# Attention and two feed-forward layers on one core: early tiles and weight pieces in another order, and a block's first products behind all reads of their PSUM tile

## Chip, core and metric

The kernel runs on one core of a Trainium2 chip. The metric is the device time of one execution in microseconds; the median of three runs before the change is 1276.29 us.

## What is computed

The reference takes q, k and v of shape (8, 8, 576, 64). It does three things, one after the other:

```python
# 1. attention inside chunks of 64 positions
attn = softmax(q_c @ k_c.T / 8); out = attn @ v_c
x = out.transpose(0, 2, 1, 3).reshape(8, 576, 512)
# 2. norm, two products with a ReLU between, residual (w_ch1: 512 x 2048, w_ch2: 2048 x 512)
xn = (x - mean) / sqrt(var + 1e-6) * g_ln
x = x + relu(xn @ w_ch1) @ w_ch2
# 3. product, gelu, norm of one half, mixing along the sequence, gate, product, residual
h = gelu(x @ w_in); u, v = halves of h
x = x + (u * (w_sg @ norm(v) + b_sg)) @ w_out
```

## The kernel before, in words

The 4608 rows of x are 36 tiles of 128 rows. Steps 1 and 2 run first, for all tiles; step 3 follows. The change touches steps 1 and 2 alone.

**Tiles and blocks.** attention(t) makes one tile: two loads (q and k, then v), products of 64x64 (L295), row maxima, exponential, transposes (L305), products with v (L314), and the division (L344), which writes x. norm(t) makes the normed tile and splits it into a high half (16 bits, scalar engine, L381) and a low half (the rest, L383), which a DMA transpose writes to xT. Two tiles make a block; there are 18 blocks (NB) of 256 rows.

**Weights.** w1 and w2 come in 8 pieces each (j = 0 to 7), stored as 64-bit numbers: load_raw() loads a piece of 1 MB (two buffers, `straw`), f64() makes 32-bit numbers of it (L398 on the scalar engine, L403 on the vector engine). For w1, make_w1() finds the largest value (L424 on the scalar engine or absmax on the vector engine), sends it over all partitions with two tiny products (par(): L206, L218), scales the piece (L446 on the scalar engine or L452 on GpSimd) and splits it into halves w1h (L457) and w1l (L459). For w2 the halves are made once all 8 maxima are there (scale_w2, split_w2).

**Products.** Every product is three products of 16-bit halves (high x high, high x low, low x high). ff1(b, f) is one of 16 units of the first layer for block b, 12 products at L536, read out by L540 and L541; a w1 piece feeds two units of each block, so four while blocks 0 and 1 are done together. ff2(b, f) (L557) is the second layer. These plain forms serve blocks 0 to 3. Blocks 4 to 17 use ff1p and ff2p (L640 and L689), which save products by sums and differences of quarters: ff2p(b, j) makes seven groups of three products, P1, P6, P5, P7, P2, P3, P4 in this order, each in a half bank of PSUM. P1 and P6 are the two halves of one bank, P5 and P7 those of another, and both banks are one tile, pair[0]. P2 and P3 share a bank (bank[6]), P4 lies in bank[7]. All seven add up over the eight units j = 0 to 7 of a block; then copy(1), stt(6), copy(5), stt(7) and stt(2), stt(3), stt(4) read them out (copy is L712 on the scalar engine, stt is L707 on the vector engine), and the unit j = 0 of the next block starts the same banks again.

**What sets the order.** All of this is not issued as written. Each step is given to a planner by op(engine, ns, function, rd, wr, prio, lat). run() keeps a clock for each engine, takes the step that can start first, the one with the smallest prio among those that are ready, and issues it; ns is the time that the planner believes a step takes, lat what it adds before another engine may use the result. So the table TUNE (the prio of tiles in `a`, of w1 pieces in `w`, of w2 pieces in `w2`; the engine of steps in `lo`, `wl`, `wc`, `wa`, `wm`) and the numbers ns set the order of the instructions of each engine, and the hardware runs each engine's list in that order. Where the planner sees TensorE idle before a step, busy() issues products of a tile of zeros (L970), whose result nobody reads. The waits between engines are put in by the framework from what each instruction reads and writes, in the order in which they were issued. It follows whole tiles: a write to any part of pair[0] waits for the reads of pair[0] that were issued ahead of it, and a read waits for the writes that were issued ahead of it.

## Time and profile before

| | |
|---|---|
| three runs | 1274.23, 1276.29, 1277.38 us; median 1276.29 |
| the profiled execution | 1274.01 us, span 1272.2 us, mean granted TensorE clock 0.993 |
| busy: TensorE, vector, scalar, GpSimd | 96%, 65%, 46%, 39% of the span |
| steps 1 and 2; step 3 | up to 866.95 us; from there to the end |
| first product of the first layer | 38.62 us |

The trace has one row for each instruction or for a few equal ones: start and length in microseconds, engine, line, what is written and read, and in brackets the idle time of the engine just before it with what ended it. PE is TensorE, DVE the vector engine, ACT the scalar engine, POOL GpSimd, SP the engine that issues the DMAs. A product on PE is shown as busy until its last result is out, so products that follow each other closely overlap in the rows, and the sum of a stretch can hide small losses.

### The profile page before, as it was taken

To read this page: it belongs to the slowest core of one execution; us is meant where nothing else is said; L and a number is where in the kernel's file an instruction comes from. 1 tells how busy PE (TensorE), PEld (TensorE's weight loads), DVE (VectorE), ACT (ScalarE), POOL (GpSimd) and SP (SyncE) were. 2 spreads that over 40 slices of the span, in tenths; PEclk is the share of its full clock that TensorE was granted. 3 is DMA by queue.
4 is the path that set the end of the run, shared out by engine and by line. 5 is a ranking of instruction groups with operands and counts; after the bars stand their busy time and mean duration, and the time that the engine had idled before them with its cause. 6 is when DMAs were issued, how large, how long until landed. Compare 5 with 4: busy or idle time off the path is not lost.

```text
span 1272.2 us, 26588 instructions
## 1 busy us (share of the span) xinstructions
PE 1218.5 (96%) x11119; PEld 872.5 (69%) x11119; DVE 825.1 (65%) x1621; ACT 586.5 (46%) x963; POOL 491.2 (39%) x446
## 2 busy tenths in 40 slices
PE   6889999988999999999999999999999999999998
PEld 4677654667888888888888888884544554554553
DVE  7885125995766656555555665546979579669665
ACT  5775402545834533333334333535736626526530
POOL 3341401644656544434444344233434144233220
PEclk9999999989999999999999999999999999999999
DMA  9954002246312221222132120612030331331102
GB/s 303 261 172 120 1 26 67 74 149 181 101 51 68 51 73 48 66 67 67 52 67 60 51 59 18 156 28 91 9 68 33 116 59 42 125 59 42 50 1 75
DMA packets 106392, 102.05 MB, mean 80 GB/s; under 512 B 79648, under 2 KB 79648, under 8 KB 106272
## 3 DMA queue, kind: packets, MB, share of 16 engines
q1 hardware_dynamic: 106272, 100.36, 28.2%
q8 instruction: 87, 1.43, 0.5%
q14 instruction: 33, 0.27, 0.1%
HBM read 62.59 MB, written 18.87 MB: 64 GB/s over the span
## 4 chain that ended last, share of the span: by engine, by line
PE 75%; DVE 14%; ACT 3%; DMA 3%; POOL 2%; issue 2%; SPq 0%; DVEq 0%; ACTq 0%; POOLq 0%
PE bank L640 20%; PE pair L689 11%; PE bank L689 8%; PE pb L1105 8%; PE pb L1087 7%; PE pb L1167 6%; PE pair L557 3%; PE pb L1043 3%; PE bank L536 3%; PE bank L557 2%; DMA straw<-in_w 2%; DVE gl L249 1%; PE pair L295 1%; DVE tf L600 1%; PE pb L1106 1%
## 5 line engine op out<-in xcount | busy, mean ns | idle before, releaser
L640 PE MATMUL bank<-xT,w1h 128*128 128x256 f16 x1792 | 301.6, 273 | 0.0
L689 PEld LDWEIGHTS <-arena 128*128 128x128 f16 x2352 | 226.7, 98 | 46.0 <-issue 17.0
L640 PE MATMUL bank<-xT,w1l 128*128 128x256 f16 x896 | 245.0, 273 | 0.0
L669 POOL TENSOR_TENSOR arena<-arena 128x896 f16<-128x896 f32 x69 | 130.2, 1886 | 255.6 <-ACT arena L667 255.5
L667 ACT ACTIVATE arena<-arena 128x896 f16<-128x896 f32 x112 | 106.3, 949 | 204.7 <-PE bank L689 131.4
L640 PEld LDWEIGHTS <-w1h 128*128 128x128 f16 x1792 | 175.3, 98 | 21.7 <-issue 0.5
L662 DVE TENSOR_TENSOR arena<-arena 128x256 f32<-128x256 f32 x112 | 63.6, 568 | 149.1 <-ACT arena L655 146.9
L655 ACT ACTIVATE arena<-bank 128x512 f32<-128x512 f32 x112 | 66.6, 595 | 123.7 <-PE bank L640 122.5
L689 PE MATMUL pair<-w2s,arena 128*128 128x256 f16 x672 | 110.6, 274 | 10.3 <-DVE u L707 6.8
L689 PE MATMUL pair<-w,arena 128*128 128x256 f16 x672 | 111.0, 274 | 2.7 <-DVE u L707 1.3
L1119 POOL TENSOR_TENSOR uT<-uT,vs 128x512 f32<-128x512 f32 x32 | 49.0, 1533 | 151.6 <-DVE vs L1115 151.6
L1043 PE MATMUL pb<-win,x2T 128*128 128x512 f16 x432 | 96.8, 379 | 1.5 <-DVE x L707 1.5
L640 PEld LDWEIGHTS <-w1l 128*128 128x128 f16 x896 | 87.9, 98 | 10.4
L1087 PE MATMUL pb<-x2T,win 128*128 128x384 f16 x576 | 94.6, 326 | 0.0
L689 PE MATMUL bank<-w,arena 128*128 128x256 f16 x672 | 93.7, 274 | 0.0
L536 PE MATMUL bank<-xT,w1h 128*128 128x256 f16 x512 | 86.1, 273 | 6.7 <-DVE latel L541 2.9
L1105 PE MATMUL pb<-wsg,vh 128*128 128x512 f16 x288 | 88.0, 380 | 0.0
L1167 PE MATMUL pb<-wout,gh 128*128 128x512 f16 x288 | 85.7, 379 | 1.9 <-DVE x L1172 1.9
L1087 PEld LDWEIGHTS <-win 128*128 128x128 f16 x576 | 56.2, 98 | 37.5
L717 POOL TENSOR_TENSOR x<-x,u 128x256 f32<-128x256 f32 (+1 forms) x60 | 64.4, 1089 | 44.3 <-ACT arena L667 30.8
L1024 DVE SCALAR_TENSOR_TENSOR q<-q,h 128x384 f32<-128x384 f32 (+1 forms) x84 | 51.3, 614 | 39.0 <-ACT q L1022 39.0
L1043 PEld LDWEIGHTS <-x2T 128*128 128x128 f16 x432 | 41.3, 98 | 50.9 <-issue 2.7
(225 smaller groups left out, 2332.5 us busy)
## 6 DMA issues: line engine op xcount, KB each, us to landing
straw<-in_w SPq DMA_DIRECT2D x16, 1023.8 KB, 6.6
qkl<-in_qkv SPq DMA_DIRECT2D x26, 512.0 KB, 3.8
x2d<-x SPq DMA_DIRECT2D x36, 256.0 KB, 2.0
x<-x2d SPq DMA_DIRECT2D x36, 256.0 KB, 4.4
out<-x SPq DMA_DIRECT2D x36, 256.0 KB, 2.0
vl<-in_qkv SPq DMA_DIRECT2D x26, 256.0 KB, 2.7
qk<-in_qkv SPq DMA_DIRECT2D x10, 512.0 KB, 5.7
raw<-in_w_in SPq DMA_DIRECT2D x4, 1023.8 KB, 5.6
```

Source lines behind the costliest of these rows:

```text
L536: nc.tensor.matmul(acc, lhsT=w[j][:, k, fc], rhs=xT.t[:, x, k], start=(n == 0), stop=(n == 11))
L557: nc.tensor.matmul(acc[i], lhsT=h[x].t[:, c], rhs=w2t[j][:, f % 2, y], start=(f == 0 and n == 0), stop=(f == NF - 1 and n == 2),)
L640: nc.tensor.matmul(acc[:, y * 256:y * 256 + 256], lhsT=w[j][:, k, fc], rhs=xT.t[:, x, k], start=(n == 0), stop=(n == 11),)
L655: op("ACT", 600, lambda: nc.scalar.activation(out=o.t[:, 0:4].rearrange("p n t -> p (n t)"), in_=acc, func=AF.Relu, scale=0.5), rd=[kb] + ...
L667: op("ACT", 950, lambda: nc.scalar.activation(out=h.t[:, 0], in_=o.t[:, 1:8], func=AF.Copy), rd=[o] + ar, wr=[h], prio=-100)
L669: op(lo[0], lo[1], lambda: lo[2].tensor_tensor(out=h.t[:, 1], in0=o.t[:, 1:8], in1=h.t[:, 0], op=ALU.subtract), rd=[o], wr=[h], prio=-100)
L689: nc.tensor.matmul(acc, lhsT=h.t[:, x, n], rhs=r(y), start=(first and j == 0 and m == 0), stop=(j == 7 and m == 2), skip_group_check=True,)
L717: op("POOL", ns, lambda: nc.gpsimd.tensor_tensor(out=d(), in0=d(), in1=v(), op=ALU.add), rd=u, wr=[x], prio=-50)
L1043: nc.tensor.matmul(ps, lhsT=x[:, k, c], rhs=w[:, k, 512:1024], start=(n == 0), stop=(n == 11))
L1087: nc.tensor.matmul(ps, lhsT=w[:, k, fc], rhs=x[:, k, c], start=(n == 0), stop=(n == 11))
L1105: nc.tensor.matmul(ps, lhsT=v[:, fc], rhs=w[:, 0:512], **f)
L1167: nc.tensor.matmul(ps, lhsT=x[:, k, c], rhs=w[:, k], start=(n == 0), stop=(n == 11))
```

## The change

It has four parts, all of them in what the planner is told.

1. Other numbers in TUNE: other prio of tiles 0 to 7 and of all weight pieces, and other engines. The scaling of w1 pieces 3, 4 and 7 moves from the scalar engine to GpSimd (`wc`); the low halves of pieces 2, 3 and 6 move from the vector engine to GpSimd and that of 7 the other way (`wl`); the maximum of w1 piece 2 moves to the scalar engine (`wa`); of the w2 maxima those of pieces 0, 3 and 7 change their engine, so that five instead of six are on the vector engine (`wm`); the low halves of tiles 4, 6 and 7 move to the vector engine (`lo`).
2. Other believed times ns (the first tiles now use the table COST too).
3. OWN: the first product of a block, P1 at j = 0, is also a write of P6, P5 and P7 to the planner, and P2 one of P3. So it stands behind all four reads of pair[0].
4. The reads of a block's sums are given other dependencies among each other (the names q1, q6, q5, q7), without the long lat of 1200.

```diff
-    a=[-270, -85, -10, -65, -85, -10, -145, 0],
+    a=[-465, -3175, 30, -50, -95, 25, -3470, 1760],
...
-    wl=[0, 0, 1, 1, 0, 0, 1, 0],
-    wc=[0, 1, 0, 0, 0, 1, 1, 0],
+    wl=[0, 0, 0, 0, 0, 0, 0, 1],
+    wc=[0, 1, 0, 1, 1, 1, 1, 1],
...
-            if not early:
-                ns = COST.get((eng, ns), ns)
+            ns = COST.get((eng, ns), ns)
...
-        op("ACT", 260, lambda: nc.scalar.activation(out=h[0].t, in_=acc, func=AF.Relu), rd=[kb], wr=[h[0]], prio=-100)
+        op("ACT", 370, lambda: nc.scalar.activation(out=h[0].t, in_=acc, func=AF.Relu), rd=[kb], wr=[h[0]], prio=-100)
...
+    OWN = {1: ["P6", "P5", "P7"], 2: ["P3"]}
...
-            op("PE", 326, lambda p=p: mm(p), rd=[h, f"w2_{j}"], wr=[f"P{p}"] + extra, prio=1000 + nff[0])
+            op("PE", 326, lambda p=p: mm(p), rd=[h, f"w2_{j}"], wr=[f"P{p}"] + extra + OWN.get(p, []) * (j == 0), prio=1000 + nff[0])
...
-            def stt(p, c, out, add, n=0):
+            def stt(p, c, out, add, x, rd=()):
...
-                ), rd=[f"P{p}", f"P{3 if p == 2 else p}"], wr=u if n else [x1 if p == 4 else x0], prio=-120, lat=1200)
+                ), rd=[f"P{p}", *rd], wr=[x], prio=-120)
...
-            copy(1, ca, 0)
-            stt(6, cb, lambda: U(1), lambda: U(0), 1)
-            copy(5, cb, 2)
-            stt(7, cb, lambda: U(3), lambda: U(1), 3)
+            copy(1, ca, 0, ["P1", "P6"], u + ["q1"])
+            stt(6, cb, lambda: U(1), lambda: U(0), "q6", ["q1"])
+            stt(7, cb, lambda: U(3), lambda: U(1), "q7", ["q6"])
+            copy(5, cb, 2, ["P5", "P7", "q1"], ["q5"])
```

The lines of the changed kernel are shifted: L689 is L690 there, L707 is L708, L712 is L713, and lines between about 240 and 670 are one less.

Three places show what moves. The first is TensorE around a boundary of two blocks (from block 8 to 9). pair_63 is the tile pair[0], w_7 and w_0 are pieces of w2, w2s are sums made of them; P1 and P5 read w, P6 and P7 w2s; L314 (L313) belongs to a tile of attention. Before:

```order
L689 MATMUL pair_63<-w2s_2496,arena 128x256
L314 MATMUL pair_64<-vl,pt 64x64 [waits DMAHW7_49,Activation_49]
L689 MATMUL pair_63<-w_7_166,arena 128x256 [waits Activation_49]
...
L689 MATMUL pair_63<-w_0_159,arena 128x256 [waits Activation_49]
...
L689 MATMUL pair_63<-w2s_2489,arena 128x256 [waits DVE_49]
```

Now:

```order
L313 MATMUL pair_64<-vl,pt 64x64 [waits DMAHW7_49,Activation_49]
...
L690 MATMUL pair_63<-w_7_166,arena 128x256
...
L690 MATMUL pair_63<-w2s_2552,arena 128x256 [waits Activation_49]
...
L690 MATMUL pair_63<-w_0_159,arena 128x256 [waits DVE_49]
...
L690 MATMUL pair_63<-w2s_2545,arena 128x256
```

In the last unit of the old block the attention product stood between P6 and P5, and P5 waited for copy(1); now it stands ahead of P1, and P7 waits for copy(1). In the new block P6 waited for the vector engine (stt(7), issued behind P1); now P1 does, and P6 waits for nothing. The first pattern stands at seven boundaries (from block 8 to block 15), the second at all 13.

The second place is the vector engine at the same kind of boundary. Before, stt(7) stood last, behind a step of the next block (L669):

```order
L707 SCALAR_TENSOR_TENSOR u<-pair_63,c_c2b,u 128x256 [waits Activation_49]
L707 SCALAR_TENSOR_TENSOR x<-bank_67,c_c2a,x 128x256 [waits PE_49]
L707 SCALAR_TENSOR_TENSOR x<-bank_68,c_c2n,x 128x256 [waits PE_49]
L707 SCALAR_TENSOR_TENSOR x<-bank_67,c_c2a,x 128x256
L669 TENSOR_TENSOR arena<-arena 128x896 [waits Activation_49]
L707 SCALAR_TENSOR_TENSOR u<-pair_63,c_c2b,u 128x256 [waits PE_49,Activation_49]
```

```order
L708 SCALAR_TENSOR_TENSOR u<-pair_63,c_c2b,u 128x256 [waits PE_49,Activation_49]
L708 SCALAR_TENSOR_TENSOR u<-pair_63,c_c2b,u 128x256 [waits Activation_49]
L708 SCALAR_TENSOR_TENSOR x<-bank_67,c_c2a,x 128x256 [waits PE_49]
L708 SCALAR_TENSOR_TENSOR x<-bank_68,c_c2n,x 128x256 [waits PE_49]
L708 SCALAR_TENSOR_TENSOR x<-bank_67,c_c2a,x 128x256
L668 TENSOR_TENSOR arena<-arena 128x896 [waits Activation_49]
```

Now the two reads of pair[0] stand first and next to each other, and stt(7) no longer waits for TensorE's product of the new block.

The third place is GpSimd in the first part (w1l is the low half of a w1 piece, hl that of a tile, cw<-cw the scaling of a piece). Before:

```order
L452 TENSOR_SCALAR cw_334<-cw_334,gsw_139 128x256 x4
...
L459 TENSOR_TENSOR w1l1_152<-cw_334,w1h1_144 128x1024
L383 TENSOR_TENSOR hl_591<-xn_581,hl_591 128x512
L459 TENSOR_TENSOR w1l0_151<-cw_271,w1h0_143 128x1024
...
L459 TENSOR_TENSOR w1l4_155<-cw_788,w1h4_147 128x1024
...
L452 TENSOR_SCALAR cw_878<-cw_878,gsw_139 128x256 x4
L459 TENSOR_TENSOR w1l5_156<-cw_878,w1h5_148 128x1024
```

Now:

```order
L451 TENSOR_SCALAR cw_386<-cw_386,gsw_139 128x256 x4
L458 TENSOR_TENSOR w1l1_152<-cw_386,w1h1_144 128x1024
L458 TENSOR_TENSOR w1l0_151<-cw_309,w1h0_143 128x1024
...
L451 TENSOR_SCALAR cw_685<-cw_685,gsw_139 128x256 x4
L451 TENSOR_SCALAR cw_887<-cw_887,gsw_139 128x256 x4
L458 TENSOR_TENSOR w1l3_154<-cw_685,w1h3_146 128x1024
L451 TENSOR_SCALAR cw_947<-cw_947,gsw_139 128x256 x4
L458 TENSOR_TENSOR w1l4_155<-cw_887,w1h4_147 128x1024
```

The low halves of pieces 1 and 0 now follow each other directly, and from piece 3 on GpSimd scales each piece as well as halving it, with the scaling of the next piece ahead of the low half of this one. The number of products with zeros on TensorE goes from 55 to 108.

## Rows read from the trace of the kernel before

**Rows 1.** The page: span, and busy time of TensorE and the vector engine.

```profile
span 1272.2 us, 26588 instructions
PE 1218.5 (96%) x11119; PEld 872.5 (69%) x11119; DVE 825.1 (65%) x1621; ACT 586.5 (46%) x963; POOL 491.2 (39%) x446
```

**Rows 2.** Waits of TensorE: total us, times, longest.

```profile
PE pair L689 <- DVE u L707: 8.1, 12, 1.0
PE pair L295 <- DVE x L344: 8.1, 5, 2.6
...
PE pair L689 <- DVE x L707: 0.6, 1, 0.6
```

**Rows 3.** Stretches: length, busy time of PE, PEld, DVE, ACT, POOL, granted clock.

```profile
0.00:38.62 38.62, 25.95 (x432) 18.59 (x433) 28.18 (x63) 23.39 (x43) 16.51 (x28) 0.91 0.97 311
38.62:45.33 6.71, 4.57 (x93) 3.65 (x90) 6.21 (x18) 2.25 (x6) 4.40 (x6) 1.00 1.01 160
45.33:126.50 81.17, 72.76 (x758) 60.40 (x759) 60.30 (x136) 57.14 (x121) 20.93 (x21) 1.00 0.58 174
126.50:220.00 93.50, 93.50 (x590) 52.26 (x588) 26.08 (x49) 21.68 (x35) 17.35 (x13) 1.00 0.11 32
```

**Rows 4.** TensorE: all products with zeros as a group, and one row of ten.

```profile
L970 PE MATMUL bank<-zero 128*128 128x256 bf16 x55 | 11.3, 358 | 1.9 <-DVE zero L875 1.0 <-issue 0.9
...
46.65 1.25 PE L970 MATMUL bank<-zero 128*128 128x256 bf16 x10
```

**Rows 5.** Timeline of all engines at one boundary of blocks, 566 to 574 us.

```profile
566.66 0.49 PE L689 MATMUL pair<-w,arena 128*128 128x256 f16 x3
...
566.99 0.49 PE L689 MATMUL pair<-w2s,arena 128*128 128x256 f16 x3
...
567.52 0.47 ACT L712 ACTIVATE u<-pair,c_c2a 128x256 f32<-128x256 f32 x1
...
568.04 0.49 PE L689 MATMUL pair<-w,arena 128*128 128x256 f16 x3
...
572.30 0.49 PE L689 MATMUL pair<-w,arena 128*128 128x256 f16 x3
...
572.90 0.48 DVE L707 SCALAR_TENSOR_TENSOR u<-pair,c_c2b,u 128x256 f32<-128x256 f32 x1 [1.00 <-PE pair L689]
...
573.44 0.49 PE L689 MATMUL pair<-w2s,arena 128*128 128x256 f16 x3 [0.65 <-DVE u L707]
```

**Rows 6.** TensorE, two places where P7 waits for copy(1).

```profile
300.24 0.49 PE L689 MATMUL pair<-w2s,arena 128*128 128x256 f16 x3 [1.76 <-ACT u L712]
...
787.55 0.49 PE L689 MATMUL pair<-w2s,arena 128*128 128x256 f16 x3 [0.56 <-ACT u L712]
```

**Rows 7.** Groups up to 125 us, vector and scalar engine: busy us, mean ns.

```profile
L459 DVE TENSOR_TENSOR w1l<-cw,w1h 128x1024 f16<-128x1024 f32 x3 | 3.7, 1222 | 1.1 <-ACT w1h L457 1.0
L201 DVE TENSOR_REDUCE mxw<-cw 128x4 f32<-128x1024 f32 x3 | 3.6, 1194 | 0.0
L432 DVE TENSOR_TENSOR mxw<-mxw,g1s 128x4 f32<-128x4 f32 x3 | 1.7, 556 | 0.0
...
L446 ACT ACTIVATE cw<-cw,gsw 128x256 f32<-128x256 f32 x20 | 8.5, 498 | 1.3 <-DVE gsw L440 1.3
```

**Rows 8.** Timeline of GpSimd and, last, of the vector engine, 27 to 38 us.

```profile
27.71 1.85 POOL L452 TENSOR_SCALAR cw<-cw,gsw 128x256 f32<-128x256 f32 x4 [1.73 <-DVE gsw L440]
...
34.19 1.15 POOL L383 TENSOR_TENSOR hl<-xn,hl 128x512 f16<-128x512 f32 x1
35.30 2.13 POOL L459 TENSOR_TENSOR w1l<-cw,w1h 128x1024 f16<-128x1024 f32 x1
...
36.09 1.37 DVE L432 TENSOR_TENSOR mxw<-mxw,g1s 128x4 f32<-128x4 f32 x1
```

**Rows 9.** Timeline of SP: issues of the last eight loads of weights.

```profile
68.40 31.19 SPq L391 DMA_DIRECT2D straw<-in_w  x7
102.21 0.37 SPq L391 DMA_DIRECT2D straw<-in_w  x1
```

More of the change, by code (lines that the diff above doesn't have):

```diff
@@ L397, in f64 @@
         dst = dst or (lambda: w.t)
-        op("ACT", 950 if pr < 9000 else 1350, lambda: nc.scalar.activation(
+        op("ACT", 1350, lambda: nc.scalar.activation(
             out=top.t.bitcast(F16).rearrange("p (n w) -> p n w", w=2)[:, :, 1],
@@ L402, in f64 @@
         ), rd=[raw], wr=[top], prio=pr)
-        op("DVE", 1140, lambda: nc.vector.scalar_tensor_tensor(
+        op("DVE", 1210, lambda: nc.vector.scalar_tensor_tensor(
             out=dst().bitcast(U32), in0=raw.t.rearrange("p (n w) -> p n w", w=2)[:, :, 0], scalar=13,
@@ L440, in scale @@
             nc.vector.tensor_scalar(out=gs, in0=g1s, scalar1=inv, scalar2=8.0, op0=ALU.mult, op1=ALU.mult)
-        op("DVE", 520, scale, wr=[f"e{j}"], prio=pr)
+        op("DVE", 690, scale, wr=[f"e{j}"], prio=pr)
         def mul():
@@ L456, in make_w1 @@
         op(("ACT", "POOL")[TUNE['wc'][j]], (1620, 1840)[TUNE['wc'][j]], mul, rd=[f"e{j}"], wr=[w], prio=pr)
-        op("ACT", 950, lambda: nc.scalar.activation(out=w1h[j], in_=wv(), func=AF.Copy), rd=[w], wr=[f"w1h{j}"], prio=pr)
+        op("ACT", 1050, lambda: nc.scalar.activation(out=w1h[j], in_=wv(), func=AF.Copy), rd=[w], wr=[f"w1h{j}"], prio=pr)
         lo = ("DVE", 1140, nc.vector) if TUNE['wl'][j] else ("POOL", 2100, nc.gpsimd)
@@ L539, in ff1 @@
         op("PE", 1285, mm, rd=[xT, f"w1h{j}", f"w1l{j}"], wr=[kb], prio=pr)
-        op("ACT", 260, lambda: nc.scalar.activation(out=h[0].t, in_=acc, func=AF.Relu), rd=[kb], wr=[h[0]], prio=-100)
-        op("DVE", 340, lambda: nc.vector.scalar_tensor_tensor(
+        op("ACT", 370, lambda: nc.scalar.activation(out=h[0].t, in_=acc, func=AF.Relu), rd=[kb], wr=[h[0]], prio=-100)
+        op("DVE", 415, lambda: nc.vector.scalar_tensor_tensor(
             out=h[1].t, in0=acc, scalar=0.0, in1=h[0].t, op0=ALU.max, op1=ALU.subtract
@@ L704, in ff2p, with copy @@
             U = lambda n: u[n // 2].t[:, n % 2 * 256:n % 2 * 256 + 256]
-            def stt(p, c, out, add, n=0):
+            def stt(p, c, out, add, x, rd=()):
                 op("DVE", 480, lambda: nc.vector.scalar_tensor_tensor(
                     out=out(), in0=POS[p][0], scalar=c, in1=add(), op0=ALU.mult, op1=ALU.add
-                ), rd=[f"P{p}", f"P{3 if p == 2 else p}"], wr=u if n else [x1 if p == 4 else x0], prio=-120, lat=1200)
-            def copy(p, c, n):
-                op("ACT", 380, lambda: nc.scalar.activation(
+                ), rd=[f"P{p}", *rd], wr=[x], prio=-120)
+            def copy(p, c, n, rd, wr):
+                op("ACT", 470, lambda: nc.scalar.activation(
                     out=U(n), in_=POS[p][0], func=AF.Copy, scale=c
-                ), rd=[f"P{p}", f"P{p + 5 if p == 1 else 7}"], wr=[u[n // 2]], prio=-120, lat=1200 if n else 300)
+                ), rd=rd, wr=wr, prio=-120)
             def add(x, d, v, ns):
@@ L718, in add @@
                     out=d(), in0=d(), in1=v(), op=ALU.add
[L719 to L732 removed]
+                ), rd=u + ["q6", "q5", "q7"], wr=[x], prio=-50)
+            copy(1, ca, 0, ["P1", "P6"], u + ["q1"])
+            stt(6, cb, lambda: U(1), lambda: U(0), "q6", ["q1"])
+            stt(7, cb, lambda: U(3), lambda: U(1), "q7", ["q6"])
+            copy(5, cb, 2, ["P5", "P7", "q1"], ["q5"])
+            stt(2, ca, lambda: half(x0, 0), lambda: half(x0, 0), x0, ["P3"])
+            stt(3, ca, lambda: half(x0, 1), lambda: half(x0, 1), x0)
+            stt(4, cn, lambda: half(x1, 0), lambda: half(x1, 0), x1)
+            add(x0, lambda: x0.t, lambda: u[0].t, 1400)
+            add(x1, lambda: half(x1, 0), lambda: U(3), 850)
+            add(x0, lambda: half(x0, 1), lambda: U(2), 850)
+            add(x1, lambda: half(x1, 1), lambda: U(3), 850)
+            add(x1, lambda: half(x1, 1), lambda: U(2), 850)
             for t, x in ((2 * b, x0), (2 * b + 1, x1)):
```

23 lines of the change are left out of this document (7 added, 16 removed).

## The prediction

> **What bounds the kernel now.** I read the page's busy shares first: TensorE is busy for 1218.5 of 1272.2 us, no other engine over 65% [rows 1]. So I looked next at what TensorE waits for, summed by cause [rows 2], and then at where those waits lie, by a table of stretches [rows 3]. The reader should see three things. First, the total idle time of TensorE is only 53.7 us; a change of order can win no more than that, plus part of the 11.3 us in which TensorE multiplies the tile of zeros [rows 1, 4]. Second, one cause repeats: the first products of a block (L689) wait for the vector engine's reading of the block before (L707), 8.1 us in 12 waits and 0.6 us once more [rows 2]. Third, the rest is early: 12.7 us idle before the first real product at 38.62 us, 2.1 us up to the first product of block 1 at 45.33, 8.4 us from there to 126.5, and none from 126.5 to 220 [rows 3, 4].
>
> The granted clock is 0.91 in the stretch to 38.62 us and 1.00 in the three behind it [rows 3], so the loss from the lower level of TensorE's clock (1.2 instead of 2.4 GHz) lies there too.
>
> **The boundaries of the blocks.** There are 13 (blocks 5 to 17). Rows 5 show one. P1, the first product of the new block, starts at 572.30; only behind it may stt(7), the last read of the old block's sums in the same tile, run (572.90), and only behind that P6 (573.44): TensorE sits idle for 0.65 us. In the changed order P1 itself stands behind all reads, P6 no longer waits, and nothing is left between stt(7) and P1: in that row set copy(1) starts at 567.52, and the four reads take 0.47 or 0.48 us each, so with gaps of about 0.1 they end near 570, over 2 us ahead of P1. The 13 waits are worth 8.7 us idle. Each also breaks the overlap of groups: a group of three is busy for 0.49 us, but they follow each other by 0.33 (566.66, 566.99) [rows 5], so 0.16 us more is lost each time, 2.1 us in all. **Gain: 10.8 us.**
>
> The order shows what is given back. Before, in seven boundaries an attention product (L314) stands between P6 and P5 of the last unit, and the wait of P5 for copy(1) passes underneath it: 567.52 + 0.47 is 567.99, P5 starts at 568.04, with no idle time [rows 5]. Now that product stands ahead of P1, and the wait for copy(1) has moved to P7 of the same unit, with nothing to cover it. A row has this price: where P7 waits for copy(1) already, the idle time is 0.56 us (787.55) [rows 6]. With the lost overlap 0.72 us; seven times, **5.0 us back**. Net: -5.8 us. The ends: -10.8 if the scalar engine is done early enough each time, and +2.6 if each new wait is as long as the longest of its kind, 1.76 us at 300.24 [rows 6] (7 x 1.92 = 13.4). I take 0.56, because in rows 5 copy(1) starts as soon as P6 has ended (566.99 + 0.49 is 567.48), so the scalar engine was free.
>
> A rule speaks for the first of these ends: the Trainium skill, PSUM — Partial Sum Buffer, section "PSUM bank collisions raise a hardware error", asks for a guard by bank, not by address. P1 and P7 lie in different banks of the pair tile; by that rule P7 would need no wait for copy(1), and the boundaries would give 10.8. The row at 787.55 shows the wait all the same, so I keep 5.0.
>
> **The start.** Counted with the rows of the stretch to 125 us [rows 7]: the vector engine loses two lower halves of w1 (2 x 1.22), one maximum over a w1 piece (1.19 + 0.56) and one over a w2 piece, as wide, 1.19, and gets three lower halves of tiles 4, 6 and 7; no row shows these there, half of the 1.22 for twice the width is the nearest, 1.8 in all. That is -3.6 us. The scalar engine loses three multiplications (8.5 us for 20 rows, 0.42 each, four to a piece, so 1.7) and gets a maximum over a w1 piece and one over a w2 piece; as an estimate by width I take 1.7 for the first, the multiplication's own, and 1.2 for the second, the vector engine's 1.19 for such a pass: -2.2 us. GpSimd gets three multiplications (1.85) and two lower halves of w1 (2.13), and loses three of tiles (1.15): +6.4 us [rows 8]. If the vector and scalar work all lay on the path, 5.8 us would go. GpSimd is not the limit by rate: 1.85 + 2.13 = 3.98 us per piece, against the four units of TensorE that a piece feeds, 5.24 us (12 products at 0.109, from 0.33 for three).
>
> The first product: the lower half of w1 piece 0 ends at 35.30 + 2.13 = 37.43, with a tile's lower half (34.19, 1.15 us) between it and piece 1's [rows 8]; that one now stands behind, so the product can come 1.2 us earlier. But the third product needs tiles 2 and 3, whose path is no shorter; I leave it at 45.33. What goes, goes behind that: of the 10.5 us idle between 38.62 and 126.5 I take **5 us** as gone, about what the two engines are relieved of. The ends: -10.5, all of it; and +6.6, from the 53 further products with zeros (108 for 55), which cost nothing while TensorE would wait anyway; ten take 1.25 us [rows 4], so with no cover 53 x 0.125 is 6.6. SP's loads are the same in number; that of w1 piece 2 now stands behind four loads of q, k and v, and the last eight still follow each other by the 4.8 us of (102.21 - 68.40) / 7 [rows 9].
>
> From the last products of block 2's ff2 to the first boundary the vector engine's order is the old one, row for row; the 8.1 us of waits on L344 [rows 2] stay, and the last stage is untouched: 0.
>
> **Sum.** -5.8 - 5.0 = -10.8 us. The profiled execution took 1274.01 us, 1.8 us over its span; that gives 1263.2. The median of the three runs is 1276.29, 2.3 us above it, and I forecast the median: **1265.5 us**.
>
> **The rivals.**
> A. The start gives nothing, because the third product and the loads set it: then only the boundaries count, 1276.3 - 5.8 = 1270.5. For it: the last eight loads follow each other no faster than one in 4.8 us [rows 9], nearly the 5.24 us in which TensorE uses a piece up. Chance 0.17.
> B. The new waits at P7 are hidden: -10.8 - 5.0, 1260.5. Chance 0.10.
> C. The boundaries only change their wait: +2.6 - 5.0 = -2.4, 1273.9. It needs the scalar engine busy when P6 ends, as at 300.24; against it, it was free at that time in rows 5. Chance 0.06.
> D. GpSimd's added work holds up the vector engine. Seen here: the product of two tiny tiles (L432) took 1.37 us from 36.09 and ended as GpSimd's lower half did (35.30 to 37.43); the mean of the three such products is 0.56 [rows 7, 8]. If each of the five added GpSimd instructions holds a vector instruction for its whole length, 3 x 1.85 + 2 x 2.13 = 9.8 us, the start costs 4.8, and the sum is -1.0: 1275.3. The Trainium skill says so in SBUF — State Buffer, section "Who interferes with whom": a vector instruction with two SBUF inputs and a GpSimd instruction that reads SBUF exclude each other. The row at 36.09 agrees. But most of these pieces lie where the vector engine runs maxima and reads from PSUM, so the chance is 0.06.
> E. Slower: GpSimd's queue. The multiplication of piece 4 now stands ahead of the lower half of piece 3, that of piece 5 ahead of 4's. If the scale of the next piece comes more than 5.24 us behind its own, TensorE stops; with one load interval of 4.8 us lost for each of pieces 3, 4 and 5, that is 14.4, and 14.4 - 5.8 = +8.6: 1284.9. For it: GpSimd works in order, and what it gets is more than any engine loses. Against it: its 3.98 us per piece leave 1.26 of the 5.24. Chance 0.06.
>
> **How the numbers follow.** My case has 0.55, with 1261 to 1270 of its own (the start between -9.5 and -0.5). About 0.3%, 3.8 us, is what a measurement of this kernel can tell, so faster begins below 1272.5: mine, A and B, 0.82. Within: C and D, 0.12. Slower: E, 0.06. The range of 8 in 10 goes from 1257 to 1274: it takes in A, B and C and leaves out D, E and the far end of B.
>
> **What would show it.** Right: in the waits of TensorE the line of stt() is gone from the block's first products, and seven to eleven waits of about 0.56 us on the scalar engine's copy stand at P7; between the third product and the first ff2 the idle time is near 3.4 us instead of 8.4; from there to the first boundary nothing differs. Wrong: waits at P1 of over 0.2 us (the reads end too late); vector instructions of 0.2 us that take 1 to 2 us in many places (D); TensorE waiting at L535 for the transfer or GpSimd's lower half w1l (E); products with zeros that run while a real one was ready.

## The result and the profile after

The changed kernel took 1261.57 us (median of four runs, 1258.21 to 1264.11) against 1275.26 us for the kernel before, run beside it: a ratio of 0.989, 95% interval 0.9857 to 0.9924. That is 13.7 us less; the forecast was 10.8 us less, and 1265.5 us. A second comparison (change_again, below) gave 1260.35 against 1272.2, a ratio of 0.9909 (0.9894 to 0.9924), 11.9 us less. The changed kernel differs by 1.2 us between the two comparisons, the kernel before by 3.1: beside all later runs it took 1271.8 to 1272.7 us, so 13.7 is the upper end. The profiled execution of the change has a span of 1262.3 us, 9.9 less than that of before.

The page of the changed kernel, and the waits of TensorE by cause (total us, times, longest):

```profile
span 1262.3 us, 26714 instructions
PE 1221.2 (97%) x11172; PEld 874.2 (69%) x11172; DVE 843.5 (67%) x1619; ACT 587.0 (47%) x961; POOL 498.3 (39%) x457
```

```profile
PE pair L690 <- ACT u L713: 6.1, 10, 1.2
PE bank L535 <- DMA xT<-hl: 3.4, 1, 3.4
...
PE pb L1044 <- DVE x L708: 2.0, 1, 2.0
...
PE pair L690 <- ACT x L713: 1.5, 2, 0.9
```

The 13 waits for stt() of [rows 2] are gone. In their place the waits for copy() have grown from six (four and two) to twelve (ten and two). The stretches between the same events as in [rows 3] (length, busy time of PE, PEld, DVE, ACT, POOL, granted clock) are these:

```profile
0.00:34.75 34.75, 26.39 (x427) 18.28 (x428) 23.57 (x54) 21.35 (x46) 12.47 (x23) 0.85 0.92 308
34.75:48.27 13.52, 9.54 (x158) 7.08 (x155) 10.09 (x27) 7.70 (x13) 5.81 (x11) 1.00 1.02 264
48.27:125.70 77.43, 74.83 (x787) 63.00 (x788) 59.30 (x135) 53.52 (x110) 30.57 (x32) 1.00 0.57 168
```

The first product of the first layer comes 3.9 us earlier, the first one of block 1 (the third unit) 2.9 us later, and TensorE's idle time from there to the first product of ff2 falls from 8.4 to 2.6 us. That first product of ff2 comes only 0.8 us earlier (126.50 and 125.70), but by then 612 products of the first layer are done instead of 576, three units more, and the next stretch of ff2 is shorter by them (41.68 and 37.76 us; before, then now):

```profile
126.50:168.18 41.68, 41.68 (x290) 28.17 (x288) 8.33 (x19) 16.91 (x28) 13.56 (x7) 1.00 0.00 1
```

```profile
125.68:163.44 37.76, 37.76 (x255) 24.66 (x253) 7.49 (x17) 16.20 (x26) 13.77 (x7) 1.00 0.00 1
```

To divide the whole, I take two marks: the start of the last product of ff2 in blocks 0 to 3, and that of the last product of block 17. They stand in the view of one line's instructions (shortest, median and longest duration in ns, then first and last start). Of the kernel before:

```profile
L557 PE MATMUL bank<-w,arena x96: 379/379/634, 211.5 to 238.6; 128*128 128x512 f16 x96
```

```profile
L689 PE MATMUL bank<-w2s,arena x336: 272/273/283, 249.2 to 865.2; 128*128 128x256 f16 x168
```

Of the change:

```profile
L556 PE MATMUL bank<-w,arena x96: 379/379/634, 206.8 to 233.6; 128*128 128x512 f16 x96
```

```profile
L690 PE MATMUL bank<-w2s,arena x336: 272/273/421, 244.5 to 853.1; 128*128 128x256 f16 x168
```

So the start is 5.0 us shorter (238.6 to 233.6), the blocks take 619.5 instead of 626.6 us (-7.1), and from the last product of block 17 to the end it is 409.2 instead of 407.0 (+2.2). All kernels of this study by the same marks, each from its one profiled execution, with the medians of the runs:

| kernel | start, to | blocks take | rest takes | span | median | before, beside it | ratio, 95% |
|---|---|---|---|---|---|---|---|
| before | 238.6 | 626.6 | 407.0 | 1272.2 | | | |
| the change | 233.6 | 619.5 | 409.2 | 1262.3 | 1261.57 | 1275.26 | 0.9857 to 0.9924 |
| change_again | 232.0 | 618.9 | 409.3 | 1260.2 | 1260.35 | 1272.20 | 0.9894 to 0.9924 |
| start_only | 229.2 | 629.2 | 407.1 | 1265.5 | 1268.74 | 1272.47 | 0.9961 to 0.9980 |
| bound_only | 238.3 | 618.8 | 409.2 | 1266.3 | 1267.64 | 1272.47 | 0.9945 to 0.9974 |
| swap_tiles | 232.7 | 613.1 | 407.0 | 1252.8 | 1252.89 | 1272.47 | 0.9833 to 0.9867 |
| before_swap | 237.6 | 613.1 | 407.4 | 1258.1 | 1262.35 | 1272.47 | 0.9905 to 0.9936 |
| last_reads | 231.8 | 619.9 | 407.0 | 1258.7 | 1260.52 | 1272.20 | 0.9890 to 0.9922 |
| no_zeros | 231.1 | 621.7 | 407.5 | 1260.3 | 1261.11 | 1272.20 | 0.9899 to 0.9928 |
| old_engines | 246.4 | 619.9 | 409.2 | 1275.5 | 1277.62 | 1272.20 | 1.0031 to 1.0056 |
| old_order | 234.3 | 620.8 | 407.5 | 1262.6 | 1263.99 | 1271.79 | 0.9924 to 0.9954 |
| old_scaling | 232.6 | 620.1 | 407.5 | 1260.2 | 1263.78 | 1271.79 | 0.9924 to 0.9950 |
| first_behind_reads | 238.1 | 617.1 | 407.2 | 1262.4 | 1264.68 | 1271.79 | 0.9916 to 0.9954 |
| old_reads | 228.6 | 617.0 | 407.1 | 1252.7 | 1255.93 | 1272.73 | 0.9853 to 0.9886 |

The first column needs care: six kernels issue the same instructions up to that mark (the change, change_again, start_only, swap_tiles, last_reads and old_reads) and reach it between 228.6 and 233.6 us, 231.3 on average. The four with the old start (before, bound_only, before_swap, first_behind_reads) reach it between 237.6 and 238.6. The start's gain is therefore 6.8 us on average and 4 to 10 us in a single pair. The second and third column repeat better: 619.5 and 618.9, 409.2 and 409.3 for the same kernel.

### The profile page after: what moved, and what is told of

It is laid out like the page before. It is cut to its first block, busy times and chain, and to the rows that moved or that the text cites. A ratio compares the mean times of both kernels' runs of the same rounds, so it can differ in the third digit from the quotient of the medians.

```text
span 1262.3 us, 26714 instructions
## 1 busy us (share of the span) xinstructions
PE 1221.2 (97%) x11172; PEld 874.2 (69%) x11172; DVE 843.5 (67%) x1619; ACT 587.0 (47%) x961; POOL 498.3 (39%) x457
## 4 chain that ended last, share of the span: by engine, by line
PE 81%; DVE 11%; DMA 4%; ACT 3%; issue 1%; POOL 0%; SPq 0%; DVEq 0%; ACTq 0%; POOLq 0%
PE bank L639 22%; PE pair L690 11%; PE bank L690 8%; PE pb L1106 8%; PE pb L1088 7%; PE pb L1168 6%; PE bank L535 5%; PE pair L556 3%; PE pb L1044 3%; PE bank L556 2%; DMA straw<-in_w 2%; DVE gl L249 1%; PE pair L294 1%; PE pair L313 1%; DVE tf L599 1%; DMA qk<-in_qkv 1%
## 5 line engine op out<-in xcount | busy, mean ns | idle before, releaser
L690 PEld LDWEIGHTS <-arena 128*128 128x128 f16 x2352 | 228.4, 98 | 37.9 <-issue 9.5
L661 DVE TENSOR_TENSOR arena<-arena 128x256 f32<-128x256 f32 x112 | 74.6, 666 | 100.7 <-ACT arena L654 100.5
L690 PE MATMUL pair<-w2s,arena 128*128 128x256 f16 x672 | 110.6, 274 | 7.1 <-ACT u L713 5.7
L690 PE MATMUL pair<-w,arena 128*128 128x256 f16 x672 | 110.6, 274 | 0.5 <-ACT u L713 0.5
L690 PE MATMUL bank<-w,arena 128*128 128x256 f16 x672 | 92.3, 274 | 0.0
L535 PE MATMUL bank<-xT,w1h 128*128 128x256 f16 x512 | 86.0, 273 | 6.1 <-DMA xT<-hl 3.4
L1088 PEld LDWEIGHTS <-win 128*128 128x128 f16 x576 | 56.2, 98 | 37.6
```

Source lines behind the costliest of these rows:

```text
L535: nc.tensor.matmul(acc, lhsT=w[j][:, k, fc], rhs=xT.t[:, x, k], start=(n == 0), stop=(n == 11))
L661: nc.vector.tensor_tensor(out=two(6, 8), in0=two(1, 3), in1=two(0, 2), op=ALU.subtract)
L690: nc.tensor.matmul(acc, lhsT=h.t[:, x, n], rhs=r(y), start=(first and j == 0 and m == 0), stop=(j == 7 and m == 2), skip_group_check=True,)
L1088: nc.tensor.matmul(ps, lhsT=w[:, k, fc], rhs=x[:, k, c], start=(n == 0), stop=(n == 11))
```

## The experiments

**The two halves of the change, each alone.** start_only leaves out the third and fourth part, that is, the whole function ff2p() is the old one; bound_only leaves out the first and second, so that ff2p() alone is the new one. The core of start_only against the change:

```diff
-    OWN = {1: ["P6", "P5", "P7"], 2: ["P3"]}
...
-            copy(1, ca, 0, ["P1", "P6"], u + ["q1"])
-            stt(6, cb, lambda: U(1), lambda: U(0), "q6", ["q1"])
-            stt(7, cb, lambda: U(3), lambda: U(1), "q7", ["q6"])
-            copy(5, cb, 2, ["P5", "P7", "q1"], ["q5"])
+            copy(1, ca, 0)
+            stt(6, cb, lambda: U(1), lambda: U(0), 1)
+            copy(5, cb, 2)
+            stt(7, cb, lambda: U(3), lambda: U(1), 3)
```

> The change without its third and fourth part: the new table and the new believed times, but the reads and the first products of a block as before. Theory (start and boundaries are two separate gains): the last product of ff2 comes about 4.9 us earlier than before, as in the profile of the change (233.6 for 238.6), TensorE waits at the boundaries as before (13 waits of about 0.65 us on stt(), 8.7 us), and the time is about 5 us under before, near 1270.5. Rival (the gain of the start is lost again at the first boundaries, or the start moves only work about): 1274 to 1276, and step 3 begins as late as before.

Measured: 1268.74 us, 3.7 less than before. The start is 9.4 us shorter in its profile, but the blocks take 629.2 us, 2.6 more than before. Among the waits of TensorE those for the reads have grown: the longest for stt() is 1.6 us (1.0 in [rows 2]), the longest for copy() 2.0 us (1.76 in [rows 6]):

```profile
PE pair L688 <- DVE u L706: 8.3, 12, 1.6
PE pair L688 <- ACT u L711: 4.7, 4, 2.0
```

So the theory holds for the start, and the rival in part: some of the gain is given back at the boundaries to blocks 6 and 7, where these long waits stand (2.00 us at 337.76, 1.06 at 387.58, 1.58 at 390.60). Of the 2.6 us, some 1.5 lie there and some 1.1 ahead of the first product of block 4 (8.7 us behind the mark in before, 9.8 here).

> The kernel before with the third and fourth part of the change alone. Theory: no difference up to the last product of ff2 at about 238.6; from the first product of block 4 to the last of block 17 about 7.4 us less than before (610.6 for 618.0 in the two profiles); no waits on stt(), seven to eleven of 0.56 us on copy(1) at P7; time about 1268. Rival C of the prediction (the boundaries only change their wait): 1274 or more.

Measured: 1267.64 us, 4.8 less. Up to the first mark no product stands in another place (238.3 for 238.6), the blocks take 7.8 us less, and eleven waits for copy() of 0.56 us stand there, none for stt(). Rival C falls. What was not expected is the last column, 2.2 us more at the end, which comes with this half and not with the other.

**What P7 waits for.** The same exchange of tiles, on the change and on the kernel before:

```diff
-        1: (pair[0][:, 0, 0:256], True), 6: (pair[0][:, 0, 256:512], False),
-        5: (pair[0][:, 1, 0:256], True), 7: (pair[0][:, 1, 256:512], False),
-        2: (bank[6][:, 0:256], True), 3: (bank[6][:, 256:512], False), 4: (bank[7][:, 0:256], True),
+        1: (bank[6][:, 0:256], True), 6: (bank[6][:, 256:512], False),
+        5: (bank[7][:, 0:256], True), 7: (bank[7][:, 256:512], False),
+        2: (pair[0][:, 0, 0:256], True), 3: (pair[0][:, 0, 256:512], False), 4: (pair[0][:, 1, 0:256], True),
```

> The change, with the tiles of the seven sums exchanged: P1 and P6 in bank[6], P5 and P7 in bank[7], P2, P3 and P4 in pair[0]. No order and no engine changes, but P7 (and P5) no longer share a tile with P1, so nothing ties them to copy(1). Theory (the wait at P7 is for the whole tile alone): all ten waits on the scalar engine's copy go, 7.6 us idle and 0.16 us of overlap each, so about 9 us under the change, near 1252.5. Rival (the wait stands for something real, such as the scalar engine's reading of the sums at the same time, and comes back in longer products or at another one): less than 3 us under the change, with products of over 0.33 us spacing while copy(1) runs.

Measured: 1252.89 us, close to the theory's 1252.5; 19.6 less than before where the change is 11.9 to 13.7 less. Timeline of the boundary from block 10 to 11 in the change, the one of [rows 5]: the attention product (L313), then P1, P6 and P5 of the last unit, copy(1), P7, and at 562.66 and 562.99 P1 and P6 of the new block:

```profile
556.39 0.69 PE L313 MATMUL pair<-vl,pt 64*64 64x64 f32 x32
...
557.02 0.50 PE L690 MATMUL pair<-w,arena 128*128 128x256 f16 x3
...
557.36 0.49 PE L690 MATMUL pair<-w2s,arena 128*128 128x256 f16 x3
...
557.68 0.49 PE L690 MATMUL pair<-w,arena 128*128 128x256 f16 x3
...
558.21 0.47 ACT L713 ACTIVATE u<-pair,c_c2a 128x256 f32<-128x256 f32 x1 [1.06 <-PE pair L690]
...
558.74 0.49 PE L690 MATMUL pair<-w2s,arena 128*128 128x256 f16 x3 [0.56 <-ACT u L713]
...
562.66 0.49 PE L690 MATMUL pair<-w,arena 128*128 128x256 f16 x3
...
562.99 0.49 PE L690 MATMUL pair<-w2s,arena 128*128 128x256 f16 x3
```

The same place with the exchanged tiles:

```profile
553.53 0.50 PE L690 MATMUL bank<-w,arena 128*128 128x256 f16 x3
...
553.87 0.49 PE L690 MATMUL bank<-w2s,arena 128*128 128x256 f16 x3
...
554.20 0.49 PE L690 MATMUL bank<-w,arena 128*128 128x256 f16 x3
...
554.40 0.47 ACT L713 ACTIVATE u<-bank,c_c2a 128x256 f32<-128x256 f32 x1 [0.73 <-PE bank L690]
...
554.52 0.49 PE L690 MATMUL bank<-w2s,arena 128*128 128x256 f16 x3
```

In the change P7 begins 1.06 us behind P5; with the tiles exchanged it begins 0.32 behind it, under the running copy(1) (554.40 to 554.87), and no product is longer for it. The blocks take 613.1 us, 6.4 less than in the change. The wait at P7 belongs to the tile. The Trainium skill (PSUM — Partial Sum Buffer, "PSUM bank collisions raise a hardware error") asks for a guard by bank; P7 and copy(1) use different banks in both kernels, and here the run without the wait agrees with it. The other 2.2 us of the profile are the head of step 3 (407.0 for 409.2, below).

> The kernel before with nothing but the same exchange of tiles; its order of reads and first products stays as it was. Theory: P6 no longer waits for stt(7), because stt(7) reads bank[7] and neither waits for P1 nor holds P6; the waits on stt() (8.7 us idle, 2.1 of overlap) and those on copy() (4.1 us idle, 1.0 of overlap) all go: about 15 us under before, near 1260, as much as the whole change brings. Rival (a new wait of P5 for stt(7), which is issued behind P1, takes the place of that of P6): 13 waits at P5 of 0.3 us or more, and the time 1266 or more.

Measured: 1262.35 us, 10.1 less than before; the blocks take 613.1 us, 13.5 less. The theory holds for the place and not quite for the size: of all waits at boundaries two are left, 1.1 and 0.7 us. The profiled execution took 1259.89 us, 2.5 less than the median of this kernel, and that of before 1274.01, 1.5 more than the median beside it, so the two profiles differ by more than the medians. This one edit of three lines, with the old order and the old reads, brings nearly as much as the whole change.

**The change again, and the head of step 3.** change_again is the change itself; last_reads alters one read:

```diff
-            stt(7, cb, lambda: U(3), lambda: U(1), "q7", ["q6"])
+            stt(7, cb, lambda: U(3), lambda: U(1), "q7", ["q6"] + ["P3"] * (b == NB - 1), -110 if b == NB - 1 else -120)
```

> The change itself once more, beside the three edits of it below. Theory (three terms that add up: start, boundaries, first products of step 3): if the sum of the profiles holds, 10 us under before; -3.7 of the run of the first two parts alone and -4.8 of the last two alone make -8.5. Rival (something further that the profiles don't show made the first comparison 13.7 us): over 12 us under before.

Measured: 1260.35 us, 11.9 less than before, nearer the rival's bound than the theory's numbers. The profiles do account for it: the average start (-6.8), the blocks (619.2 on average, -7.4) and the rest (+2.2) make -12.0. The halves alone make only 8.5. Part of the difference is the 1.5 us that start_only lost at two boundaries, which the new place of P1 does away with (617.0 in old_reads, below); the rest is not shown.

> The change, with stt(7) of the last block alone put behind stt(2), stt(4) and stt(3), as it stood before; nothing else moves but two additions of GpSimd behind it. Theory (in the last block stt(7) waits for copy(5) on the same tile, so the vector engine ends 0.44 us later, TensorE waits 1.96 instead of 1.52 us, and its first products of step 3 then run at the lower clock): the wait is 1.5 us, the first 24 products take about 5.4 us instead of 7.0, and the time is about 2 us under the change. Rival (the lower clock there is chance): no wait longer than 1.6 us, but the 24 products take 7 us as before, and under 1 us is won.

Measured: 1260.52 us, no different from change_again: by the whole time the theory is not confirmed. At the place itself its first half, the wait, is. In the last block of the change, the vector engine's last reads:

```profile
853.54 0.48 DVE L708 SCALAR_TENSOR_TENSOR x<-pair,c_c2b,x 128x256 f32<-128x256 f32 x1 [0.54 <-ACT x L713]
...
854.72 0.48 DVE L708 SCALAR_TENSOR_TENSOR x<-bank,c_c2a,x 128x256 f32<-128x256 f32 x1
```

stt(7) waits 0.54 us for copy(5), and everything behind it is later. The first products of step 3 in the change and in last_reads:

```profile
855.34 9.62 PE L1044 MATMUL pb<-win,x2T 128*128 128x512 f16 x36 [1.96 <-DVE x L708]
```

```profile
853.45 7.93 PE L1044 MATMUL pb<-win,x2T 128*128 128x512 f16 x36 [1.52 <-DVE x L708]
```

The wait is 0.44 us shorter and the same 36 products take 7.93 instead of 9.62 us, so the rest takes 407.0 instead of 409.3 us. The granted clock goes with it, in stretches from the first of these products on, of the change and of last_reads:

```profile
855.30:865.00 9.70, 9.66 (x38) 3.98 (x38) 3.36 (x6) 3.15 (x6) 3.58 (x5) 0.82 0.58 200
```

```profile
853.40:863.00 9.60, 9.55 (x45) 4.22 (x46) 4.44 (x9) 4.71 (x8) 3.99 (x7) 1.00 0.56 186
```

In the change part of the stretch runs at the lower of the two levels. That this fall comes from the longer wait is not shown: no_zeros, old_order and old_scaling wait 1.96 us at this place too and run these products at the upper level, in 7.93 us. The 2.3 us of one profile do not show in the median of the runs, where the start alone spreads by 5 us.

**The products with zeros.** In no_zeros the planner issues none behind the first 14:

```diff
             nff[1] = 1
+            plan.idle = None
```

> The change without the products with zeros behind the first 14 (94 of 108 are left out; no output depends on them). Theory (they fill only time in which TensorE would wait): the first real products are not earlier, the granted clock of the first 40 us falls, and the time is 0 to 3 us longer. Rival (they stand in the way of real products): the last product of ff2 comes 2 us or more earlier and the time falls as much.

Measured: 1261.11 us, within the range of change_again (1259.32 to 1261.94). The rival falls: the time is no shorter, and the start ends at 231.1 us, within the spread of the change's. As in the theory, the first product of the first layer is not earlier (34.56 us; 34.75 and 34.09 in the change), and the clock is lower. The windows hide the clock: they give 1.00 for the first 35 us, but the clock records of this trace begin at 37.6 us only, and time without a record counts as 1.00 (so it does in the 0.91 of [rows 3], whose records begin at 20.5). The products of q and k tell it, here and in change_again (shortest, median and longest in ns):

```profile
L294 PE MATMUL pair<-qk x64: 262/311/363, 28.6 to 31.0; 64*64 64x64 f32 x64
```

```profile
L294 PE MATMUL pair<-qk x64: 218/218/267, 28.1 to 30.3; 64*64 64x64 f32 x64
```

Their median is 311 ns where the records show the lower level (before, 32 us) and 218 at the upper one. So at 28 to 31 us TensorE ran at the lower level without the products with zeros and at the upper one with them. In the whole time this is 0.8 us, within the spread. The 6.6 us that I had set as a bound for their cost is out.

**Which part of the table shortens the start.** Three kernels, each the change with some rows of its table as before; old_engines has the five lists of engines:

```diff
-    lo=[0, 0, 0, 0, 1, 0, 1, 1],
-    wl=[0, 0, 0, 0, 0, 0, 0, 1],
-    wc=[0, 1, 0, 1, 1, 1, 1, 1],
-    wa=[1, 1, 1, 0, 1, 1, 1, 0],
-    wm=[1, 1, 1, 0, 1, 1, 0, 0],
+    lo=[0, 0, 0, 0, 0, 0, 0, 0],
+    wl=[0, 0, 1, 1, 0, 0, 1, 0],
+    wc=[0, 1, 0, 0, 0, 1, 1, 0],
+    wa=[1, 1, 0, 0, 1, 1, 1, 0],
+    wm=[0, 1, 1, 1, 1, 1, 0, 1],
```

old_scaling has the old `wl` and `wc` of these alone, and old_order the old `a`, `w`, `w2` and `f`.

> The change with the engine lists of the kernel before (wl, wc, wa, wm, lo), but with the new order numbers and believed times. Theory (the relief of the vector and scalar engines by 5.8 us is what shortens the start): the gain of the start is lost, the last product of ff2 comes at about 238 us, and the time is some 4 us over the change. Rival (the order alone does it): within 1.5 us of the change.

Measured: 1277.62 us, 17.3 over change_again and 5.4 over the kernel before. The order alone loses, and by four times what the theory gave. TensorE at the costliest place of old_engines:

```profile
91.40 0.61 PE L535 MATMUL bank<-xT,w1h 128*128 128x256 f16 x2 [3.16 <-ACT w1h L456]
93.62 0.40 PE L535 MATMUL bank<-xT,w1l 128*128 128x256 f16 x1 [1.61 <-POOL w1l L458]
```

This is rival E's mechanism, with the scalar engine ahead of GpSimd: a piece of w1 comes too late. These 4.8 us are a third of the loss: the start ends 14.4 us later than in change_again, and 5.0 of them are there at the third unit already, where TensorE waits for a transfer of xT (53.51 us here, 48.47 in change_again). From 90 to 98 us, around the waits for w1, the granted clock is 0.57, mostly the lower level:

```profile
53.51 0.61 PE L535 MATMUL bank<-xT,w1h 128*128 128x256 f16 x2 [3.14 <-DMA xT<-hl]
```

```profile
90.00:98.00 8.00, 4.99 (x27) 3.38 (x28) 7.96 (x10) 5.17 (x7) 4.21 (x2) 0.57 0.50 158
```

The stretch of 60 to 90 us (busy PE, PEld, DVE, ACT, POOL) shows the engine that is full, in old_engines and in change_again:

```profile
60.00:90.00 30.00, 25.99 (x246) 20.89 (x243) 23.81 (x54) 26.50 (x60) 9.94 (x10) 1.00 0.66 221
```

```profile
60.00:90.00 30.00, 30.00 (x314) 24.90 (x313) 26.38 (x62) 20.81 (x41) 22.03 (x24) 1.00 0.67 226
```

With the old lists the scalar engine is busy 26.5 of 30 us, TensorE 26.0; with the new ones GpSimd does 12 us more, the scalar engine has 20.8, and TensorE is never idle. (In the change's own profile these two are 20.6 and 28.3, in old_scaling, below, 24.5 and 27.4.)

> The change with the order numbers of the kernel before (a, w, w2 and f of TUNE), but with the new engine lists and believed times: the other half of the table. Theory after the last run (order and engines fit each other, neither half carries the gain): clearly over the change, 5 to 15 us, so 1265 to 1275, with the last product of ff2 at 237 us or later. Rival (the engines alone carry the gain): within 2 us of the change, the last product of ff2 near 232.

Measured: 1263.99 us, 3.6 over change_again; the start ends at 234.3. Less than the theory wanted, more than the rival allows: with the new lists the old order is only a little worse.

> The change with wc and wl of the kernel before alone: the scaling of w1 pieces 3, 4 and 7 again on the scalar engine, the low halves of 2, 3 and 6 again on the vector engine and that of 7 on GpSimd; wa, wm, lo and the order are the new ones. Theory (what the old engine lists cost, 17 us, is mostly this work of w1 on the scalar and vector engines): 10 to 17 us over the change. Rival (the maxima and the low halves of tiles weigh as much): under 6 us over the change.

Measured: 1263.78 us, 3.4 over change_again. The theory falls. Of the 17.3 us that the old lists cost under the new order, the scaling and the low halves of w1, which I took for the main part, put back alone cost 3.4 at most: the intervals of the two ratios touch (0.9924), and the profile's start is no longer than the change's (232.6). If the parts add up, the other 13.8 hang on `wa`, `wm` and `lo`; neither that nor which of the three carries it was tried.

**Which part of the change makes the new waits.** first_behind_reads is the kernel before with OWN alone, old_reads the change without its fourth part; the edit to the kernel before is the same in both:

```diff
+    OWN = {1: ["P6", "P5", "P7"], 2: ["P3"]}
...
-            op("PE", 326, lambda p=p: mm(p), rd=[h, f"w2_{j}"], wr=[f"P{p}"] + extra, prio=1000 + nff[0])
+            op("PE", 326, lambda p=p: mm(p), rd=[h, f"w2_{j}"], wr=[f"P{p}"] + extra + OWN.get(p, []) * (j == 0), prio=1000 + nff[0])
```

> The kernel before with the third part of the change alone: P1 of a block behind all reads for the planner, the reads in their old order among each other, the old table. Here the attention product stays between P6 and P5 of the last unit, and stt(7) stays the last read. Theory (P6's wait goes, and with stt(7) as the last read P7 of the new block waits for it, behind three groups instead of one): 13 waits of 0.1 to 0.2 us on stt(7) at P7 in place of 0.65 us at P6, no new waits on copy(1) at the seven boundaries from block 8 to 15, and the time 4 to 8 us under before, 1264 to 1268. Rival (the wait only moves and keeps its length, because stt(7) is issued later still): under 2 us won.

Measured: 1264.68 us, 7.1 less than before, inside the forecast; but not by its mechanism. The planner, which now sees P1 held back, issues P2, P3 and P4 of the new block first and P1 a unit of the first layer later (rows of the same order below). So stt(7) ended well ahead of P1, P7 of the new block waited nowhere, and the blocks take 617.1 us, 1.7 less than with both parts in bound_only.

> The change without its fourth part: the new table, the new believed times and P1 behind all reads, but the reads of the sums in their old dependencies among each other. Theory (the fourth part costs what it was not needed for: it moves the attention product away from in front of P5 at seven boundaries, 7 x 0.72 us, and makes the last read later, 2.2 us at the head of step 3): no waits on copy() at the seven boundaries from block 8 to 15, 1.52 us ahead of step 3, from the last product of ff2 to the last of block 17 about 617 us, and the time about 4 us under the change, near 1256.5. Rival (the old reads delay the first boundaries under the new believed times, as they did in the run of the first two parts alone): within 2 us of the change, with waits of over 1 us at the boundaries to blocks 5, 6 and 7.

Measured: 1255.93 us, 16.8 less than before and 4.4 less than change_again (by the table 1.9 of it in the blocks and 2.2 at the end). Its boundary, of the same block as above:

```profile
552.75 0.49 PE L690 MATMUL pair<-w,arena 128*128 128x256 f16 x3
...
553.07 0.49 PE L690 MATMUL pair<-w2s,arena 128*128 128x256 f16 x3
...
553.49 0.69 PE L313 MATMUL pair<-vl,pt 64*64 64x64 f32 x32
553.60 0.48 ACT L713 ACTIVATE u<-pair,c_c2a 128x256 f32<-128x256 f32 x1
...
554.13 0.49 PE L690 MATMUL pair<-w,arena 128*128 128x256 f16 x3
554.46 0.49 PE L690 MATMUL pair<-w2s,arena 128*128 128x256 f16 x3
```

The attention product stands between P6 and P5 again and covers copy(1) (553.60 to 554.08); P5 starts at 554.13 with no idle time, as in [rows 5]. At the head of the new block stt(7), the last read, ends at 558.38; P2, P3 and P4 come first, and P1 2.3 us behind P2, at 560.68:

```profile
557.90 0.48 DVE L708 SCALAR_TENSOR_TENSOR u<-pair,c_c2b,u 128x256 f32<-128x256 f32 x1
...
558.39 0.82 PE L690 MATMUL bank<-w,arena 128*128 128x256 f16 x6
...
559.04 0.49 PE L690 MATMUL bank<-w2s,arena 128*128 128x256 f16 x3
...
560.68 0.49 PE L690 MATMUL pair<-w,arena 128*128 128x256 f16 x3
```

At the seven boundaries from block 8 on, it is 43.90 us from the first product of a block to that of the next in before, 43.82 in the change and 43.10 in old_reads, in first_behind_reads and with the exchanged tiles: here neither the 0.72 us that the change gives back at each boundary nor the wait of before is left. So the fourth part, the new dependencies of the reads, brings no gain: it moves the attention product and makes the last read of step 2 later. (This run also sets back the believed times of copy() and of the additions on GpSimd, which the edit did not separate.) The rival has a point at the first boundaries, which keep waits of 1.14 and 1.62 us.

## Why the prediction was right, point by point

**The boundaries: forecast -5.8, measured -7.1 in the profile (-7.8 in bound_only).** Both steps came out as written. No wait for stt() is left, where 13 were worth 10.8 us; the last read ends 1.8 us ahead of P1 (560.84 and 562.66), where I had written over 2. At the seven boundaries from block 8 on, P7 waits 0.56 us for copy(1), seven times in the profile, which is the price taken from the row at 787.55 [rows 6]. From P7's wait at 558.74 to that of the next boundary at 602.56 it is 43.82 us, where the same places of before lie 43.90 apart (573.44 and 617.34): at these seven the net gain is 0.08 each, as 0.81 - 0.72 has it. The 1.3 us beyond the forecast are not of this mechanism and lie at the first boundaries: the wait of 1.76 us [rows 6] is 1.15 now, and two that I did not count are gone, one of an attention product (0.82 us) and one of 0.24 us for copy(1). A wait for copy(1) near the end that grew from 0.56 to 0.91 us, and 0.3 us ahead of block 4, go the other way.

**The argument from the rule.** I kept 5.0 us given back, against a rule that would have given 10.8 for the boundaries. The change keeps the waits, and swap_tiles, which loses them with the banks as far apart as before, shows that they are a matter of the tile. Rival B's price was right too: once the tiles are exchanged, a block at the seven boundaries is 0.72 us shorter (43.82 and 43.10), which is the price of one wait with its lost overlap; with the other waits for copy() the blocks gain 6.4 us. The measured median lies nearer to rival B's 1260.5 than to my 1265.5, but the waits that B takes away are there.

**The start: forecast -5, measured -5.0 in the profile, -6.8 on average.** The size was right by luck, since one step of its working was not. I counted the work that leaves the vector and scalar engines, 5.8 us, with the scaling and low halves of w1 as its largest part, and took that sum for the gain. The relief itself was smaller: up to the first mark the vector engine is busy 2.8 us less (138.6 and 135.8) and the scalar engine 1.2 (114.3 and 113.1), and GpSimd 7.2 more. Nor is the sum what counts: the scaling and low halves of w1, put back alone, cost 3.4 us at most (old_scaling), all lists together 17.3 (old_engines), far more than the work they move. A piece of w1 that comes too late where nothing else is ready is one such loss, the 3.16 and 1.61 us of old_engines; what makes up the rest of the 17.3 stays open. The first product came 3.9 us earlier, where I had 1.2. The third, which I left at 45.33, came at 48.27, behind a wait of 3.4 us for its transfer of xT (1.1 before); the idle time behind it fell to 2.6 us, where I had written 3.4. Behind the first product of ff2 I had nothing differ up to the first boundary; there most of the gain shows, as the three units that are done earlier.

**The last stage: forecast 0, measured +2.2.** This step failed. I read the vector engine's order at the boundaries between blocks and not at the end of block 17, where no new block follows: there stt(7) now stands ahead of the other reads and waits for copy(5), and 0.44 us are added to TensorE's wait for the last of the reads. This shows in all seven kernels with that order and the old tiles. The other 1.7 us are the lower clock, in four of the seven.

**The rivals.** A (boundaries only) falls with start_only and with the marks of the table. C falls with bound_only. D would show vector instructions held up by GpSimd. Its example, the product of two tiny tiles, is short in the change. One group got longer, the normalising of the tiles, from 534 to 696 ns on average (612 in change_again), 1.3 us in all against the 9.8 of D; whether GpSimd is the cause was not tested. GpSimd's own low halves of w1 got a little longer (2133 ns on average before). The groups up to 125 us (busy us, mean ns), the second of the kernel before, the others of the change:

```profile
L431 DVE TENSOR_TENSOR mxw<-mxw,g1s 128x4 f32<-128x4 f32 x2 | 0.5, 246 | 0.0
```

```profile
L378 DVE TENSOR_SCALAR xn<-x,mv,rs 128x512 f32<-128x512 f32 x8 | 4.3, 534 | 0.5 <-POOL rs L373 0.4
```

```profile
L377 DVE TENSOR_SCALAR xn<-x,mv,rs 128x512 f32<-128x512 f32 x8 | 5.6, 696 | 1.0 <-POOL rs L372 1.0
L458 POOL TENSOR_TENSOR w1l<-cw,w1h 128x1024 f16<-128x1024 f32 x7 | 15.8, 2269 | 10.3 <-ACT w1h L456 10.3
```

E is not in the change, where nothing waits for w1l. Of its sign, a wait at L535 for the transfer, there is the one of 3.4 us, for a tile's xT and not for a piece of w1. Its mechanism is real all the same: old_engines has it, with 3.16 and 1.61 us at one place, and is slower than before.

## What to carry to other kernels

Where a product waits for a read of another bank, look at which tile both belong to: laying out the same sums so that those read first share no tile with those written next won 7.5 to 10 us here without making an instruction longer, and the order around it mattered less (613.1 us in the blocks with the old reads and with the new ones). When a dependency is put into a planner, list what slides past what because of it: the attention product that covered a wait was worth as much as the dependency was. An engine assignment and an order are one decision; half of a tuned pair can be worse than the old pair, as old_engines was (old_order, the other half, was not). The best version of this study is swap_tiles, 1252.89 us; old_reads follows with 1255.93. The two together were not tried.

## What the runs showed of the hardware that I had not expected

The granted clock at the head of step 3 follows TensorE's wait there, but not every time. After a wait of 1.96 us the 36 first products took 9.62 us and the longest of all these products 634 ns, in four kernels (the change, change_again, bound_only, old_engines); after the same wait they ran at the upper level, the longest 390 ns, in no_zeros, old_order and old_scaling. After waits of 1.45 to 1.84 us they ran at the upper level in all six others and in the kernel before. What decides in the first seven stays open.

The scalar engine's copy(5) began in the change only when the vector engine's stt(6) had ended, and stt(7) only when copy(5) had; with P1 and P6 in one tile and P5 and P7 in another, copy(5) ran beside stt(6) (555.05 to 555.52 beside 554.90 to 555.38). Reads of one tile by two engines follow each other, too, in these kernels (copy(5) sat idle 1.17 us for stt(6), stt(7) 0.54 us for copy(5)).

Six executions of the same first 230 us of instructions differ by up to 5 us at their end, more than most edits of the start are worth; a judgement on such an edit needs more than one profile. Part of it is the clock: in the change and in last_reads the last products before the mark run at the lower level (the longest 634 ns), in old_reads none do; what else makes it up was not tested.
